# Attention over recurrent segments: E left unnormalised, outputs scaled at eviction, one tile for the values, V one round later

## The chip, the cores and the metric

The kernel runs on one core of one Trainium2 chip. The metric is the device time of one execution of the whole program in microseconds (us). Engines are named as in the profile: PE (TensorE matmuls), PEld (its weight loads), DVE (VectorE), ACT (ScalarE), POOL (GpSimd) and SP (SyncE, here only issuing DMAs). PSUM is the memory that PE writes to and that DVE and ACT read from; everything else lies in SBUF or, between stages, in DRAM.

## The reference, cut

Four layers, A, B, A, B, each added to its input after a layer norm. Layer A is attention inside segments of 32 tokens, each with 8 memory rows in front; the memory rows of a segment are the first 8 output rows of the segment before. Layer B is a linear attention over the whole sequence, which the change touches only in one copy.

```python
# layer A: x [1, 2048, 640], 32 heads of 192, 8 memory rows, segments of 32
mem = mem0
for s in range(64):
    h = concat([mem, xs[s]], axis=1)                     # 40 rows
    q, k, v = h @ Wq, h @ Wk, h @ Wv                     # per head, 192 each
    scores = q @ k.T * Dh ** -0.5
    scores = where((i < 8) | (i >= j), scores, -1e9)
    p = softmax(scores)
    o = (p @ v) @ Wo                                     # 40 rows of 640
    mem = o[:, :8]
    outs.append(o[:, 8:])
```

## The kernel before

**Layer A in two stages.** The chain carries 32 rows a segment: 8 memory rows and the first 24 tokens. Q, K and V of the last 8 tokens ("tails") depend on the layer's input alone and are projected beforehand (`A_pre`) into the DRAM arrays `kqb_d` and `vb_d`; the chain adds them as extra columns and rows, since memory rows read every key. The outputs of the tails are stored to the DRAM array `otb_d` and multiplied with Wo later, within the B layer (`post_steps`).

**The chain (`A_chain`)** goes over 64 segments one after the other, since each needs the memory rows of the one before. A segment has four rounds of 8 heads, numbered 0 to 3, in falling order in every other segment, so that weights can stay; the rest of the weights streams in from DRAM over SP's queue (`load_slot`, `load_wo`, into `arena`). The block is under `tc.manual_schedule()`: each engine runs its instructions in the order in which the code issues them, and semaphores are derived from the tiles that instructions read and write.

**One round.** `project` computes Q, K and V, 20 matmuls of 128x384 each, in four column groups of the array with 32 rows each, so a bank of PSUM holds four groups of two heads. ACT copies Q and K to `raw` (L936), DVE transposes them in blocks of 32 into `QT` and `KT` (L941, L944 to L946). `scores` adds the mask by a matmul with the identity (L963) and then six products (L968). Two heads share a block of 80x80, 32 rows of each and 16 of their tails; the mask excludes what belongs to different heads, and four blocks make 80x320. `weigh` takes the exponential (ACT, L1020), `sums` multiplies with ones (L1034), so that every row holds the column sums; `normalise` takes Ln and Exp(-x) of them on ACT (L1039, L1040) and multiplies E by the result on DVE (L1041). `attend` (L976) multiplies 80 rows of the value tile `Vs[n % 2]` with E: rows 0 to 63 are the round's values, copied from PSUM by `v_rows` (L955 on ACT, L957 on DVE), rows 64 to 79 the tails' values, which `extra_v` (L909) loads by a DMA that POOL issues. The outputs fill two PSUM banks; ACT and DVE copy the round's 64 columns to `OT` (L981, L982) and the 16 tail columns to `otb` (L988 to L991), which `store_tail` (L995, POOL) writes to DRAM. `wo_round` multiplies `OT` with the round's part of Wo into the bank `W` (48 matmuls of 128x160, L1002), summed over the four rounds.

**Two value tiles.** Round n uses `Vs[n % 2]`. Behind `attend` of round n, `tails_after(n)` calls `extra_v` for round n + 2 (or the next segment's rounds 0 and 1), into the tile that this `attend` has just read. The rows 96 to 127 of the two tiles serve as buffers for the segment's input and output rows: `load_rows` (L878) brings the next 24 rows, `hx_transpose` (L882, four instructions) puts them into `hT`, `keep_rows` (L890, four) takes the outputs from `W`, `store_rows` (L893) stores them.

**Between segments** the first 8 rows of `W` go through DVE (L1145 transposes, L1146 casts) into `hT` of the next segment. `keep_busy` (L1009) issues 14 matmuls on the identity a segment, in three groups around the last two `wo_round`s; `fill` (L1015) issues weight loads without a matmul.

**Order on PE.** Q 0, K 0, V 0; then for n = 0 to 2: Q n+1, `attend` n-1, scores n, K n+1, `sums` n, `wo_round` n-1, V n+1. At the end: scores 3, half of V 3, `attend` 2, `sums` 3, the other half, `wo_round` 2, `keep_busy`, `attend` 3, `keep_busy`, `wo_round` 3, `keep_busy`. POOL's queue holds, in this order a round: `extra_v`, the four copies of `extra_kq` (L902 to L905, tails' columns into `QT` and `KT`), `load_kqb` (L897), `store_tail`.

Of the kernel before, what the change touches and what calls it, by code (L numbers as in the profile page):

```python
# [8 lines left out]
P = 128  # L9
# [12 lines left out]
SEG_FILL = 1  # L22
# [93 lines left out]
class Kernel:  # L116
# [52 lines left out]
    def run(self, layers):  # L169
# [14 lines left out]
        self.eps = const.tile([P, 1], F32, name="eps")  # L184
# [5 lines left out]
        for li, Lt in enumerate(layers):  # L190
            last = li == len(layers) - 1
            if Lt == "A":
# [3 lines left out]
                attn = dram.tile([S, Dm], BF16, name=f"attn{li}")[:]  # L196
# [355 lines left out]
    def build_A_consts(self):  # L552
        nc, const = self.nc, self.const

        mk = const.tile([P, 80], BF16, name="mask_st")
        nc.gpsimd.memset(mk[:], MASK_NEG)

        def keep(m, base, pattern, mult):  # L560
            nc.gpsimd.affine_select(out=m, in_=m, compare_op=ALU.is_ge, fill=MASK_NEG, base=base, pattern=pattern,
                                    channel_multiplier=mult)

        for G in range(2):
            for c0, c1 in ((32 * G, 32 * G + 32), (64 + 8 * G, 72 + 8 * G)):
                nc.gpsimd.memset(mk[32 * G:32 * G + 32, c0:c1], 0.0)
            keep(mk[32 * G:32 * G + 32, 32 * G + 8:32 * G + 32], 8, [[1, 24]], -1)
            for c0 in (32 * G, 64 + 8 * G):
                m = mk[64:80, c0:c0 + 8]
                nc.gpsimd.memset(m, 0.0)  # L570
                if G == 0:
                    keep(m, 7, [[0, 8]], -1)
                else:
                    keep(m, -8, [[0, 8]], 1)
                if c0 >= 64:
                    keep(m, 8 * G, [[1, 8]], -1)
        self.mk = mk
        ones = const.tile([P, 1], BF16, name="ones_blk")
        nc.vector.memset(ones[:], 1.0)
        self.ones_blk = ones  # L580

    def layer_A(self, xn_dram, at_dram, li, x_raw=None):
# [49 lines left out]
        def load_wo(r, into=None, part=range(6)):  # L632
            t = into if into is not None else wo_end[:, :] if r in (0, 3) else wo_mid[:, 7680 * (r - 1):7680 * r]
            for k in part:
                tk = t[:, 1280 * k:1280 * k + 1280]
                if r in (0, 3):
                    self.last_load = nc.sync.dma_start(out=tk, in_=self.wo_rows[r // 3, :, 1280 * k:1280 * k + 1280])
                else:
                    nc.sync.dma_start(out=tk.rearrange("p (c m) -> p c m", m=640),
                                      in_=wov[:, 12 * r + 2 * k:12 * r + 2 * k + 2, :])  # L640
# [8 lines left out]
        def lay_out_wo(i):  # L649
            nc.sync.dma_start(out=self.wo_rows[i].rearrange("p (c m) -> p c m", m=640), in_=wov[:, 36 * i:36 * i + 12, :])  # L650
# [204 lines left out]
    def A_chain(self, xn_dram, at_dram, li, load_slot, piece, load_wo, late_wo, wo_mid, wo_end, low):  # L855
# [3 lines left out]
        with tc.tile_pool(name=f"A{li}_ch", reuse_waits="tile", bufs=1) as sp, \  # L859
# [3 lines left out]
            KT = sp.tile([P, 6, 80], BF16, name="KT")  # L863
            QT = sp.tile([P, 2, 4, 80], BF16, name="QT")
            Vs = [sp.tile([P, 896], BF16, name=f"Vp{i}") for i in range(2)]
            xr, orow = [t[96:P, 0:640] for t in Vs]
            for i, t in enumerate((KT, QT, *Vs)):
                (nc.vector if i % 2 else nc.gpsimd).memset(t[:], 0.0)
            xv = xn_dram.rearrange("(s t) d -> t s d", t=32)

# [4 lines left out]
            def load_rows(s):  # L877
                nc.gpsimd.dma_start(out=xr[8:32, :], in_=xn_dram[32 * s:32 * s + 24, :])  # L878

            def hx_transpose(hT, gs):  # L880
                for g in gs:
                    nc.vector.transpose(out=hT[32 * g:32 * g + 32, :, :],  # L882
                                        in_=xr[:, 160 * g:160 * g + 160].rearrange("p (j b) -> p b j", b=KC))
# [4 lines left out]
            def keep_rows(W):  # L888
                for g in range(4):
                    nc.scalar.activation(out=orow[:, 160 * g:160 * g + 160], in_=W[32 * g:32 * g + 32, 0:160], func=ACT.Copy)  # L890

            def store_rows(s):
                nc.gpsimd.dma_start(out=at_dram[32 * s:32 * s + 24, :], in_=orow[8:32, :])  # L893
# [6 lines left out]
            def extra_kq(kqb):  # L900
                qb = kqb[:, 96:192].rearrange("p (x i q) -> p x i q", i=3, q=16)
                nc.gpsimd.tensor_copy(out=QT[:, :, 0:4:3, 64:80], in_=qb[:, :, 0:3:2, :])  # L902
                nc.gpsimd.tensor_copy(out=QT[0:64, :, 1, 64:80], in_=qb[0:64, :, 1, :])
                nc.gpsimd.tensor_copy(out=QT[64:P, :, 2, 64:80], in_=qb[64:P, :, 1, :])
                nc.gpsimd.tensor_copy(out=KT[:, :, 64:80], in_=kqb[:, 0:96].rearrange("p (c q) -> p c q", q=16))  # L905

            def extra_v(s, n):
                r = rounds(s)[n]
                nc.gpsimd.dma_start(out=Vs[n % 2][64:80, :], in_=self.vb_d[s, r].rearrange("g t f -> (g t) f"))  # L909

            def project(hT, ps, m, n, s, steps):
# [3 lines left out]
                for i in steps:  # L915
                    b = (i + KC - ns) % KC if n == 0 else i
                    w = piece(m, r, b)
                    for g in range(4):
# [6 lines left out]
                        o = ps  # L925
                        nc.tensor.matmul(o[32 * g:32 * g + 32, 0:384], lhsT=hT[:, b, :], rhs=rhs, start=(i == 0),  # L926
# [4 lines left out]
            def values(hT, n, s, pv, steps):  # L931
                project(hT, pv, "V", n, s, steps)

            def to_raw(ps, tag):
                raw = sp.tile([P, 384], BF16, name="raw", tag=tag)
                nc.scalar.activation(out=raw[:], in_=ps[:, 0:384], func=ACT.Copy)  # L936
                return raw

            def to_rows(raw, m):
                if m == "K":  # L940
                    nc.vector.transpose(out=KT[:, :, 0:64], in_=raw[:, :].rearrange("p (c j) -> p c j", j=64))  # L941
                else:
                    rv = raw[:, :].rearrange("p (x i j) -> p x i j", i=3, j=64)
                    nc.vector.transpose(out=QT[:, :, 0:4:3, 0:64], in_=rv[:, :, 0:3:2, :])  # L944
                    nc.vector.transpose(out=QT[0:64, :, 1, 0:64], in_=rv[0:64, :, 1, :])
                    nc.vector.transpose(out=QT[64:P, :, 2, 0:64], in_=rv[64:P, :, 1, :])  # L946

            def v_rows(pv, n, which="ax"):
                for x in range(2):
                    if "ax"[x] not in which:  # L950
                        continue
                    o = self.two_heads(Vs[n % 2][0:64, 448 * x:448 * x + 448])
                    i = pv[64 * x:64 * x + 64, 0:384].rearrange("p (e f) -> p e f", e=2)
                    if x == 0:
                        nc.scalar.activation(out=o, in_=i, func=ACT.Copy)  # L955
                    else:
                        nc.vector.tensor_copy(out=o, in_=i)  # L957

            def scores():

                S = pop.tile([P, 512], F32, name="ps_s", tag="s", bufs=2)
                m = self.mk[0:80, :]
                nc.tensor.matmul(S[0:80, 0:320], lhsT=self.ident[0:80, 0:80], rhs=ap3(m, [list(m.ap[0]), [0, 4], [1, 80]]),  # L963
                                 start=True, stop=False, skip_group_check=True)
                for x in range(2):
                    for i, q0, q1 in ((0, 0, 1), (1, 1, 3), (2, 3, 4)):
                        c0 = 160 * x + (80 if i == 2 else 0)
                        nc.tensor.matmul(S[0:80, c0:c0 + 80 * (q1 - q0)], lhsT=KT[:, 3 * x + i, :], rhs=QT[:, x, q0:q1, :],  # L968
                                         start=False, stop=(x == 1 and i == 2), skip_group_check=True)
                return S  # L970

            def attend(E, n):
                O = [pop.tile([P, 512], F32, name=f"ps_o{x}", tag=f"o{x}") for x in range(2)]
                for x in range(2):
                    for k, e, i in ((0, 0, 0), (320, 1, 2), (128, 0, 1), (192, 1, 1)):
                        nc.tensor.matmul(O[x][:, 80 * i:80 * i + 80], lhsT=Vs[n % 2][0:80, 448 * x + k:448 * x + k + 128],  # L976
                                         rhs=E[0:80, 160 * x + 80 * e:160 * x + 80 * e + 80], start=(k == 0),
                                         stop=(k == 192), skip_group_check=True)
                OT = sp.tile([P, 6, 64], BF16, name="OT", tag="OT")
                o = [x[:, 0:240].rearrange("p (i q) -> p i q", q=80) for x in O]  # L980
                nc.scalar.activation(out=OT[:, 0:3, :], in_=o[0][:, :, 0:64], func=ACT.Copy)  # L981
                nc.vector.tensor_copy(out=OT[:, 3:6, :], in_=o[1][:, :, 0:64])  # L982
                return OT, o

            def keep_tail(o, late=False):
                otb = sp.tile([P, 6, 16], BF16, name="otb", tag="otb", bufs=2)
                if late:
                    nc.vector.tensor_copy(out=otb[:, 0:3, :], in_=o[0][:, :, 64:80])  # L988
                else:
                    nc.scalar.activation(out=otb[:, 0:3, :], in_=o[0][:, :, 64:80], func=ACT.Copy)  # L990
                nc.vector.tensor_copy(out=otb[:, 3:6, :], in_=o[1][:, :, 64:80])  # L991
                return otb

            def store_tail(otb, s, r):
                nc.gpsimd.dma_start(out=self.otb_d[s, :, 96 * r:96 * r + 96], in_=otb[:, :, :].rearrange("p c t -> p (c t)"))  # L995

            def wo_round(W, r, OT, first, last):
                w = wo_end[:, :] if r in (0, 3) else wo_mid[:, 7680 * (r - 1):7680 * r]
                for i in range(12):
                    c, q = i % 6, 32 * (i // 6)  # L1000
                    for g in range(4):
                        nc.tensor.matmul(W[32 * g:32 * g + 32, 0:160], lhsT=OT[:, c, q:q + 32],  # L1002
                                         rhs=w[:, 640 * i + 160 * g:640 * i + 160 * g + 160], start=(first and i == 0),
                                         stop=(last and i == 11), tile_position=(0, 32 * g), skip_group_check=True)

            def keep_busy(ps, n, w=384):

                for _ in range(n):
                    nc.tensor.matmul(ps[:, 0:w], lhsT=self.ident[:, :], rhs=wo_mid[:, 0:w], start=True, stop=True,  # L1009
# [210 lines left out]
```

## Time and profile before

| what | us |
|---|---|
| runs shown | 3728.8, 3733.5, 3735.9; median 3733.5 |
| span of the profiled execution | 3735.3 |
| mean granted clock of TensorE in it | 0.980 |
| chain of the first layer A | about 209 to 1550 |
| chain of the second layer A | about 2077 to 3420 |
| a segment, start to start, mean of 126 | 21.33 |
| shortest segment | 20.91 |
| busy in the span: PE, DVE, ACT, POOL | 3544, 2368, 2073, 1659 |
| mean DMA rate | 249 GB/s |

How to read it: the span is cut at the first and last instruction of the profiled execution. "Start" of a segment is here the end of the first of the two casts that put memory rows into `hT` (L1146). In a group's line the busy sum comes first, then the mean of one instruction in ns, then the idle time of its engine just before these instructions with what ended it. Lines of the timeline give start and duration in us; what stands in square brackets is idle time before and its releaser. A matmul's duration runs over its neighbours', since they are pipelined, so prices on PE are best taken from start to start. The landing time of a DMA counts from its issue on the engine.

### The profile page before, as it was taken

The numbers are of one execution on the slowest core, as the hardware profiler recorded it, in microseconds if no ns is written. First come the engines' busy times: TensorE is split into PE (matmuls) and PEld (weight loads), VectorE is DVE, ScalarE is ACT, GpSimd is POOL, SyncE is SP. The second block draws the span as 40 slices with busy tenths as digits, with TensorE's granted clock in tenths as the row PEclk, the third lists the DMA queues.
The fourth block names the chain that finished last, engine by engine and source line by source line (L and its number), as shares of the span: only waits on it lengthen the run. The fifth ranks groups of instructions, "written<-read, shape, count | busy, mean of one in ns | idle before, by whom it ended". The sixth has DMA issues, their size and how long they took to land.

```text
span 3735.3 us, 169098 instructions
## 1 busy us (share of the span) xinstructions
PE 3543.7 (95%) x71082; PEld 2319.9 (62%) x71390; DVE 2368.0 (63%) x6330; ACT 2073.4 (56%) x5285; POOL 1658.5 (44%) x4323
## 2 busy tenths in 40 slices
PE   9999999999999999989899999999999999999898
PEld 7766666666666666545377666666666666665453
DVE  5556666666666666456633566666666666664564
ACT  2356566666666666545423566666666666665453
POOL 3345555555555555340423455455555555553400
PEclk9999999999999999989899999999999999999899
DMA  9988788888887888910377888887887888879100
GB/s 301 326 295 294 266 289 292 275 291 278 284 294 272 293 282 276 309 57 14 137 259 216 292 279 282 283 295 275 290 282 274 289 282 289 293 268 316 58 1 29
DMA packets 531381, 931.72 MB, mean 249 GB/s; under 512 B 141034, under 2 KB 298362, under 8 KB 530618
## 3 DMA queue, kind: packets, MB, share of 16 engines
q1 hardware_dynamic: 428794, 818.87, 62.6%
q0 software_dynamic: 68160, 88.78, 8.1%
q10 hardware_dynamic: 33664, 13.24, 1.4%
q8 instruction: 558, 9.14, 1.0%
q14 instruction: 205, 1.68, 0.1%
HBM read 852.43 MB, written 72.09 MB: 248 GB/s over the span
## 4 chain that ended last, share of the span: by engine, by line
PE 35%; DVE 5%; DMA 5%; ACT 4%; issue 4%; POOL 2%; PEld 2%; SPq 0%; POOLq 0%; DVEq 0%; ACTq 0%
PE ps_qk L926 9%; PE ps_w L1002 4%; PE ps_v L926 4%; PE ps_o L976 2%; PE ps_s L968 2%; PE ps_qk L389 2%; DMA arena<-wo_rows 2%; PE ps_pre L817 1%; PE ps_s L1034 1%; DVE hT L882 1%; PEld L817 1%; PE ps_s L963 1%; PE ps_idle L1009 1%; PE ps_v L419 1%; PE kv L429 1%
## 5 line engine op out<-in xcount | busy, mean ns | idle before, releaser
L926 PEld LDWEIGHTS <-hT 128*32 128x32 bf16 x30720 | 739.4, 96 | 433.1 <-DVE hT L1146 29.0
L926 PE MATMUL ps_qk<-arena,hT 128*32 128x384 bf16 x20480 | 996.3, 327 | 12.0 <-DMA arena<-in_A_Wk_dram 2.2
L936 ACT ACTIVATE raw<-ps_qk 128x384 bf16<-128x384 f32 x1024 | 503.1, 491 | 378.3 <-PE ps_s L1034 243.9
L1002 PE MATMUL ps_w<-arena,OT 128*32 128x160 bf16 x24576 | 542.7, 235 | 38.4 <-issue 22.1
L909 POOL DMA_DIRECT2D Vp<-vb x512 | 258.8, 506 | 661.6 <-PE ps_o L976 456.4
L926 PE MATMUL ps_v<-arena,hT 128*32 128x384 bf16 x10240 | 536.6, 329 | 6.6 <-DMA arena<-in_A_Wv_dram 6.6
L1002 PEld LDWEIGHTS <-OT 128*32 128x32 bf16 x24576 | 436.2, 97 | 131.1 <-issue 53.7
L941 DVE STREAM_TRANSPOSE KT<-raw 128x384 bf16<-128x384 bf16 x512 | 296.1, 578 | 195.9 <-ACT raw L936 191.9
L944 DVE STREAM_TRANSPOSE QT<-raw 128x256 bf16<-128x256 bf16 x512 | 227.9, 445 | 239.1 <-ACT raw L936 195.9
L897 POOL DMA_DIRECT2D kqb<-kqb x512 | 291.1, 569 | 173.3 <-POOL KT L905 148.2
L957 DVE CAST Vp<-ps_v 64x384 bf16<-64x384 f32 x512 | 286.2, 559 | 98.2 <-ACT Vp L955 82.7
L995 POOL DMA_DIRECT2D otb<-otb x512 | 283.0, 553 | 116.5 <-DVE otb L991 99.0
L955 ACT ACTIVATE Vp<-ps_v 64x384 bf16<-64x384 f32 x512 | 246.3, 481 | 154.2 <-PE ps_v L926 115.4
L982 DVE CAST OT<-ps_o 128x192 bf16<-128x192 f32 x512 | 183.2, 358 | 221.2 <-PE ps_o L976 203.1
L1041 DVE TENSOR_TENSOR E<-E,ps_s 80x320 bf16<-80x320 bf16 x512 | 247.5, 483 | 73.6 <-ACT ps_s L1040 69.5
L1020 ACT ACTIVATE E<-ps_s 80x320 bf16<-80x320 f32 x512 | 221.9, 433 | 126.1 <-PE ps_s L968 97.2
L976 PEld LDWEIGHTS <-Vp 80*128 80x128 bf16 x4096 | 184.3, 99 | 154.7 <-issue 120.6
L968 PE MATMUL ps_s<-QT,KT 128*80 128x80 bf16 (+1 forms) x3072 | 233.2, 213 | 24.3 <-DVE KT L941 13.4
L976 PE MATMUL ps_o<-E,Vp 80*128 80x80 bf16 x4096 | 234.5, 202 | 22.6 <-ACT Vp L955 4.2
L981 ACT ACTIVATE OT<-ps_o 128x192 bf16<-128x192 f32 x512 | 167.8, 328 | 152.6 <-PE ps_o L976 152.3
L890 ACT ACTIVATE Vp<-ps_w 32x160 bf16<-32x160 f32 x512 | 150.7, 294 | 175.0 <-DVE wt L1145 157.9
L968 PEld LDWEIGHTS <-KT 128*80 128x80 bf16 x3072 | 194.6, 119 | 73.5 <-issue 61.4
(152 smaller groups left out, 5462.5 us busy)
## 6 DMA issues: line engine op xcount, KB each, us to landing
arena<-wo_rows SPq DMA_DIRECT2D x792, 320.0 KB, 6.8
arena<-in_A_Wq_dram SPq DMA_DIRECT2D x427, 384.0 KB, 4.6
arena<-in_A_Wv_dram SPq DMA_DIRECT2D x427, 384.0 KB, 6.4
arena<-in_A_Wk_dram SPq DMA_DIRECT2D x768, 192.0 KB, 4.8
kqb<-kqb POOLq DMA_DIRECT2D x512, 48.0 KB, 5.1
arena<-in_A_Wk_dram SPq DMA_DIRECT2D x43, 384.0 KB, 7.1
vb<-arena POOLq DMA_DIRECT2D x128, 112.0 KB, 5.9
Vp<-vb POOLq DMA_DIRECT2D x512, 28.0 KB, 4.7
```

What stands on the lines that cost most here:

```text
L897: nc.gpsimd.dma_start(out=kqb[:], in_=self.kqb_d[s, :, r, :])
L909: nc.gpsimd.dma_start(out=Vs[n % 2][64:80, :], in_=self.vb_d[s, r].rearrange("g t f -> (g t) f"))
L926: nc.tensor.matmul(o[32 * g:32 * g + 32, 0:384], lhsT=hT[:, b, :], rhs=rhs, start=(i == 0), stop=(i == KC - 1), tile_position=(0, 32 * g), ...
L936: nc.scalar.activation(out=raw[:], in_=ps[:, 0:384], func=ACT.Copy)
L941: nc.vector.transpose(out=KT[:, :, 0:64], in_=raw[:, :].rearrange("p (c j) -> p c j", j=64))
L955: nc.scalar.activation(out=o, in_=i, func=ACT.Copy)
L957: nc.vector.tensor_copy(out=o, in_=i)
L968: nc.tensor.matmul(S[0:80, c0:c0 + 80 * (q1 - q0)], lhsT=KT[:, 3 * x + i, :], rhs=QT[:, x, q0:q1, :], start=False, stop=(x == 1 and i == 2 ...
L976: nc.tensor.matmul(O[x][:, 80 * i:80 * i + 80], lhsT=Vs[n % 2][0:80, 448 * x + k:448 * x + k + 128], rhs=E[0:80, 160 * x + 80 * e:160 * x ...
L995: nc.gpsimd.dma_start(out=self.otb_d[s, :, 96 * r:96 * r + 96], in_=otb[:, :, :].rearrange("p c t -> p (c t)"))
L1002: nc.tensor.matmul(W[32 * g:32 * g + 32, 0:160], lhsT=OT[:, c, q:q + 32], rhs=w[:, 640 * i + 160 * g:640 * i + 160 * g + 160], start=(firs ...
L1041: nc.vector.tensor_tensor(out=E[0:80, 0:320], in0=E[0:80, 0:320], in1=rc, op=ALU.mult)
```

## The change

It touches `A_chain`, the masks, the layout of Wo's rows in DRAM and the copies of `post_steps`.

- E is no longer multiplied by the reciprocals of the sums. `sums` now gives them on all 128 partitions, `reciprocals` puts them into the tile `rc`, and `scale_out` multiplies the outputs by `rc` as it takes them from PSUM into `OT`: one DVE product of 128x320 for columns of whole heads, two of 64x160 for the columns that two heads share. Tail columns go to `OT` with the others and `store_tail` stores them from there; `otb` is gone.
- The outputs of `attend` lie in one PSUM bank in place of two.
- There is one value tile. It holds the tail rows of rounds of even number in rows 64 to 79, those of odd number in rows 80 to 95; `scores` and `attend` work on 96 rows, and the mask, one for each parity, excludes the other's 16.
- `OT` and the columns of `QT` hold 96 and 80 places in which round columns and tail columns change sides with the parity.
- `sums` n-1, `attend` n-1 and scores n are issued in one block; V n comes behind K n+1. `wo_round` 1, 2 and 3 come at the end of the segment. `keep_busy` is gone, `SEG_FILL` is 25 in place of 1.
- Input and output rows have tiles of their own over 128 partitions, so `hx_transpose` and `keep_rows` are one instruction each; `load_rows` and `store_rows` move 32 rows in four column groups.
- The order of rows of Wo changes with that of `OT`: `lay_out_wo` is three DMAs, `load_wo` takes rows with a step, and `post_steps` copies the tails with a step of six elements.

```diff
-            Vs = [sp.tile([P, 896], BF16, name=f"Vp{i}") for i in range(2)]
-            xr, orow = [t[96:P, 0:640] for t in Vs]
+            Vs = sp.tile([P, 896], BF16, name="Vp")
+            OT = sp.tile([P, 96, 6], BF16, name="OT")
...
             def extra_v(s, n):
                 r = rounds(s)[n]
-                nc.gpsimd.dma_start(out=Vs[n % 2][64:80, :], in_=self.vb_d[s, r].rearrange("g t f -> (g t) f"))
+                t = 64 + 16 * (n % 2)
+                nc.gpsimd.dma_start(out=Vs[t:t + 16, :], in_=self.vb_d[s, r].rearrange("g t f -> (g t) f"))
...
-            def attend(E, n):
-                O = [pop.tile([P, 512], F32, name=f"ps_o{x}", tag=f"o{x}") for x in range(2)]
+            def reciprocals(S):
+                rc = sp.tile([P, 320], F32, name="rc", tag="rc")
+                nc.scalar.activation(out=S[:, 0:320], in_=S[:, 0:320], func=ACT.Ln)
+                nc.scalar.activation(out=rc[:, :], in_=S[:, 0:320], func=ACT.Exp, scale=-1.0)
+                return rc
+
+            def attend(E):
+
+                O = pop.tile([P, 512], F32, name="ps_o", tag="o", bufs=2)
                 for x in range(2):
-                    for k, e, i in ((0, 0, 0), (320, 1, 2), (128, 0, 1), (192, 1, 1)):
-                        nc.tensor.matmul(O[x][:, 80 * i:80 * i + 80], lhsT=Vs[n % 2][0:80, 448 * x + k:448 * x + k + 128],
-                                         rhs=E[0:80, 160 * x + 80 * e:160 * x + 80 * e + 80], start=(k == 0),
+                    for k, e, c in ((0, 0, 2 * x), (320, 1, 2 * x + 1), (128, 0, 4 + x), (192, 1, 4 + x)):
+                        nc.tensor.matmul(O[:, 80 * c:80 * c + 80], lhsT=Vs[0:96, 448 * x + k:448 * x + k + 128],
+                                         rhs=E[0:96, 160 * x + 80 * e:160 * x + 80 * e + 80], start=(x == 0 and k == 0),
                                          stop=(k == 192), skip_group_check=True)
+                return O
+
+            def scale_out(O, rc, n):
+                q0 = 16 - 16 * (n % 2)
+                dst = OT[:, q0:q0 + 80, :].rearrange("p q c -> p c q")
+                rv = rc[:, :].rearrange("p (x e q) -> p x e q", e=2, q=80)
+                ov = O[:, 0:480].rearrange("p (c q) -> p c q", q=80)
+                nc.vector.tensor_tensor(out=dst[:, 0:4, :], in0=ov[:, 0:4, :],
+                                        in1=rc[:, :].rearrange("p (c q) -> p c q", q=80), op=ALU.mult)
+                for e in range(2):
+                    h = slice(64 * e, 64 * e + 64)
+                    nc.vector.tensor_tensor(out=dst[h, 4:6, :], in0=ov[h, 4:6, :], in1=rv[h, :, e, :], op=ALU.mult)
+
+            def store_tail(n, s, r):
+                q0 = 80 - 80 * (n % 2)
+                nc.gpsimd.dma_start(out=self.otb_d[s, :, 96 * r:96 * r + 96],
+                                    in_=OT[:, q0:q0 + 16, :].rearrange("p q c -> p (q c)"))
...
+                for n in range(1, L):
                     raw = q_or_k("Q", n + 1)
+                    sums(S, E)
+                    O = attend(E)
+                    tails_after(n - 1)
+                    S1 = scores(n)
+                    rc = reciprocals(S)
+                    E = weigh(S1)
+                    S = S1
+                    to_rows(raw, "Q", n + 1)
                     next_kq(s, n)
...
+                        rawk = q_or_k("K", n + 1)
+                        scale_out(O, rc, n - 1)
+                        to_rows(rawk, "K")
+                    store_tail(n - 1, s, order[n - 1])
+                    pv = values(n, pop, "v")
+                    v_rows(pv, 0, "s")
+                    v_rows(pv, 1, "s")
+                    if n < L - 1:
+                        wo_round(W, order[n - 1], n == 1, False)
...
+                pv = values(L, pqp, "qk")
+                sums(S, E)
+                O = attend(E)
                 tails_after(L - 1)
+                S1 = scores(L)
                 next_kq(s, L)
+                rc = reciprocals(S)
+                E = weigh(S1)
+                v_rows(pv, 1, "v")
+                v_rows(pv, 0, "s")
+                wo_round(W, order[L - 2], False, False)
+                sums(S1, E)
+                O1 = attend(E)
+                tails_after(L)
                 if s + 1 < NSEG:
                     hT = new_hT()
-                    hx_transpose(hT, range(1))
-                wo_round(W, order[L - 1], OT, False, False)
...
+                    hx_transpose(hT, xr)
+                scale_out(O, rc, L - 1)
+                store_tail(L - 1, s, order[L - 1])
+                wo_round(W, order[L - 1], False, False)
+                rc = reciprocals(S1)
+                scale_out(O1, rc, L)
+                wo_round(W, order[L], False, True)
+                store_tail(L, s, order[L])
                 fill(SEG_FILL)
```

## The prediction

> **What bounds the kernel now.** First the page's parts 1, 5 and 6:
>
> ```profile
> PE 3543.7 (95%) x71082; PEld 2319.9 (62%) x71390; DVE 2368.0 (63%) x6330; ACT 2073.4 (56%) x5285; POOL 1658.5 (44%) x4323
> L909 POOL DMA_DIRECT2D Vp<-vb x512 | 258.8, 506 | 661.6 <-PE ps_o L976 456.4
> L1041 DVE TENSOR_TENSOR E<-E,ps_s 80x320 bf16<-80x320 bf16 x512 | 247.5, 483 | 73.6 <-ACT ps_s L1040 69.5
> L890 ACT ACTIVATE Vp<-ps_w 32x160 bf16<-32x160 f32 x512 | 150.7, 294 | 175.0 <-DVE wt L1145 157.9
> ```
>
> PE sets the time; DVE, ACT and POOL have room. In the trace the start of a segment recurs every 21.33 us (mean of both layers; the shortest took 20.91), so 128 segments are 2,730 of the 3735.3 us. The timeline of one segment, which starts at 805.63, gives the prices on PE and the place of the value tails:
>
> ```profile
> 807.32 0.99 PE L926 MATMUL ps_v<-arena,hT 128*32 128x384 bf16 x20
> 808.13 0.99 PE L926 MATMUL ps_qk<-arena,hT 128*32 128x384 bf16 x20
> 809.05 0.33 PE L963 MATMUL ps_s<-mask_st,ident 80*80 80x320 bf16 x1
> 809.35 0.45 PE L968 MATMUL ps_s<-QT,KT 128*80 128x80 bf16 x6
> 809.73 1.00 PE L926 MATMUL ps_qk<-arena,hT 128*32 128x384 bf16 x20
> ...
> 812.82 0.45 PE L976 MATMUL ps_o<-E,Vp 80*128 80x80 bf16 x8
> 813.56 0.50 POOL L909 DMA_DIRECT2D Vp<-vb  x1 [1.85 <-PE ps_o L976]
> ...
> 817.38 0.46 PE L976 MATMUL ps_o<-E,Vp 80*128 80x80 bf16 x8
> 818.13 0.51 POOL L909 DMA_DIRECT2D Vp<-vb  x1 [1.69 <-PE ps_o L976]
> ```
>
> From start to start: a projection 0.82 us, 0.92 where a full-array product follows; mask and scores 0.30 + 0.38 (the mask 0.14 behind another full-array product); by the same view `attend` 0.28, `sums` 0.26, `wo_round` 0.84 (0.94 before a full-array product), and 1.69 from the last `wo_round` to the next segment. POOL issues the next tails (L909) 0.74 us after the start of the `attend` that frees their rows (812.82 to 813.56). The waits of PE show what these loads cost today, the view of the DMA queues, narrowed to one issue at a time, how long they are under way:
>
> ```profile
> PE ps_o L976 <- DMA Vp<-vb: 4.0, 8, 1.4
> ```
>
> ```profile
> Vp<-vb POOLq DMA_DIRECT2D x1, 28.0 KB, 5.4
> ...
> Vp<-vb POOLq DMA_DIRECT2D x1, 28.0 KB, 5.9
> ...
> Vp<-vb POOLq DMA_DIRECT2D x1, 28.0 KB, 1.9
> ```
>
> These are the issues at 813.56, 818.13 and 825.61. Sorted by place over some 122 segments, the median is 5.54 us for an issue 7.9 us into the segment (9 in 10 between 4.83 and 6.03), 5.70 at 12.5 (5.39 to 6.18), 3.54 at 16.8 and 1.95 at 19.7: the weight stream fills the DMA engines until some 17 us. PE waited for them 8 times in all, since each tile is read again only two rounds later.
>
> **The change, part by part.**
>
> **One value tile.** `attend` now reads rows 0 to 95 of it, the tail rows of both parities; the mask makes the other parity's weights zero but doesn't stop the read. `extra_v` for round n+2 is still issued behind `attend` of round n, and overwrites rows that `attend` of n+1 reads. In the built program that `attend` does wait for this load's semaphore. So two successive `attend`s stand at least 0.74 + landing + about 0.05 us apart. Call them A0 to A3, in us from the segment's start, with PE's order of the new code:
> - A0: 0.05 + three projections 2.46 + V 0.92 + scores 0.68 + K 0.82 + Q 0.92 + sums 0.26 = 6.1, taken as 6.2. Issue 6.95, landing +5.5.
> - A1 = 12.55. PE's own work from A0 (attend 0.28, scores 0.52, K and V 1.64, wo 0.84, Q 0.92, sums 0.26: 4.46) would have allowed 10.7, so PE stands 1.9. Issue 13.3, landing +5.6 (between the medians at 7.9 and 12.5).
> - A2 = 18.95. Own work 0.80 + K, V, V 2.56 + sums 0.26 = 3.62 would have allowed 16.2; PE stands 2.8. Issue 19.7, landing +1.95.
> - A3 = 21.7. Own work 0.80 + wo 0.94 + sums 0.26 = 2.0 allowed 20.95; PE stands 0.75.
> - After A3: 0.28 and `wo_round` 2, 0.84, to 22.8. `scale_out` 3 overwrites the OT that it reads, so it comes after: 0.05 + its first product on 128x320. No row shows that operation; the nearest is L1041 with 0.483, the bound above a 384-element cast, L957 with 0.559. I take 0.48, as the element count is the same; the two 64-row products lie under the first two thirds of `wo_round` 3. So 23.35, and 1.69 on: the segment takes 25.1 us at full clock, 3.75 more than before.
> What queues behind the waiting `attend` on PE: the scores of the next round, hence Exp, and the next projections; POOL's own next issue waits for `attend` too, which closes the loop.
>
> **The clock.** The profile has a stall like these:
>
> ```profile
> 1333.51 0.48 PE L968 MATMUL ps_s<-QT,KT 128*80 128x80 bf16 x6 [1.94 <-POOL KT L905]
> ```
>
> ```profile
> 1331.94:1335.35 3.41, 1.84 (x35) 1.16 (x39) 0.81 (x3) 0.91 (x3) 2.54 (x8) 1.00 0.76 278
> 1335.35:1338.77 3.42, 3.42 (x71) 3.00 (x64) 1.86 (x7) 1.54 (x5) 2.39 (x7) 0.50 0.17 41
> ```
>
> PE stood 1.57 us within one stretch of 3.41, and the granted clock (third figure from the end) was 0.50 for all of the next; gaps with 1.40 us in one stretch were followed by 1.00. The 2.8 us before A2 put over 1.6 into one stretch in most positions. A half-speed stretch loses up to 1.7 us of work; behind A1 that lies in the wait for A2, behind A2 it lies on the path for `wo_round` 1 to 3 only. Bounds 0 and 1.7; I take 0.5, a third, as the place is random: 25.6 us. The removed `keep_busy` (14 matmuls a segment, in time when PE waited) costs nothing else.
> The Trainium skill, "TensorE: Matmul & The Clock Gate", section "HAM oscillation — how this bites in real kernels", allows idle gaps up to about 3.4 us; by it no gap here would lower the clock and the segment would keep the full-clock figure. The stall above, 1.94 us long, contradicts it.
> A second page speaks against the loop: by "DMA: Bandwidth & Descriptors", section "Anatomy of one DMA — SWDGE (gpsimd) path", such a load takes 2.0 us plus bytes over 436 GB/s, here 2.07; by that the waits before A1 and A2 vanish and the weight stream would decide. The landings show it for the issue at 825.61 (1.9) and not for those under the stream (5.4, 5.9).
>
> **Unnormalised E and scaling at eviction.** L1041 (0.483), four evictions and two tail copies of DVE and ACT a round give way to three products on DVE (0.48 and, from 160 elements against 320, some 0.31 twice). A round then asks DVE for 1.59 of transposes (rows L941, L944 to L946) and 1.1 of products, ACT for 3.2 (two raw copies of 0.49, two value copies of 0.48, Exp 0.43, Ln and Exp 0.83), under at least 4.5 us of PE; on the path lies the 0.53 above. Where that cover is gone, a late product costs its 0.48, four times a segment at most: 1.9. Without E in the way, scores, sums and outputs in one block save PE some 0.1 to 0.2 us a round; it goes into the waits.
>
> **V a round later, rows, masks, DMAs.** The last V no longer splits. `hx_transpose` and `keep_rows` (four of 0.294 each, L890) become one apiece, beside PE; `keep_rows` moves ahead of Q's transposes into the time of K 0, and uncovered would cost that 0.3. POOL issues as many DMAs a segment: `load_rows` moves from behind the last `attend` to K 1 and is needed only at the next segment; `store_tail` 2 and 3 come behind the issues for A2 and A3, so they delay none of these. SP's queue issues the same `wo_rows` loads at the same places; only the layout ahead of the chain takes three DMAs for one, beside the first weights. 16 more mask instructions on POOL lie there too, beside loads; each would cost under a microsecond, once, if bare. The spread copies in the later layers read with a stride of six elements: some 1.5 us a layer, 3 in all, between 0 and 10.
>
> **Sum.** 3735.3 + 128 x (25.6 - 21.33) + 3 = 3735 + 547 + 3 = 4285 us; the median of the runs shown, 3733.5, lies 2 lower, so 4283.
>
> **Rivals.**
> - **Only the weight stream binds** (faster): if all landings were as the one at 825.61, own work would set A1 and A2 and the segment would take some 20.3 us; the stream's last packet comes at 19.43 (median) and no segment ended less than 1.35 later, so 20.8: 3735 - 68 + 3 = 3670. Decides below 2.8 us of latency at A1 and 3.7 at A0. Against it: 4.83 at the lowest twentieth.
> - **The tail store binds in place of the load**: `scale_out` 3 also overwrites rows that `store_tail` 1 reads. Issued near 15.1 and, like the store at 14.8 today, 5.09 under way, it lands at 20.2; +0.53 + 1.69 gives 22.4: 3735 + 137 + 3 = 3875. It needs the value tails not to bind, against the wait in the program.
> - **Full clock**: the same loop without the gate, 25.1: 3735 + 483 + 3 = 4221.
> - **Half clock behind every A2**: 25.1 + 1.7 = 26.8: 3735 + 700 + 3 = 4438.
>
> **Numbers.** Forecast 0.56, full clock 0.16, half clock 0.16, tail store alone 0.06, stream alone 0.05, no change 0.01. Low end: both long landings 0.5 us shorter and the full clock, 24.1, gives 4090, taken as 4085; high end 4440. The spread of the runs makes 0.2% the least that can be told from no change: faster 0.05, same 0.01, slower 0.94.
>
> **What would show it.** PE waiting at the outputs' line for Vp<-vb some 5 us a segment, 600 to 700 us in all, where it was 4.0; `attend`s 6.3, 6.4 and 2.8 us apart; landings of 5.5, 5.6 and 2.0; the granted clock at 0.50 in stretches behind A2; the wait for `otb` not the last before `scale_out` 3. Wrong: landings under 4 us while the stream runs, or `attend`s that don't wait.

## The result and the profile after

The changed kernel takes 4891 us (median of 4 runs, 4879 to 4905); the kernel before 3734 (median of 4). The ratio is 1.310 with a 95% interval of 1.307 to 1.313. The profiled execution has a span of 4892.0 us and a mean granted clock of 0.873 (before 0.980). Slower was forecast, but 4283 us and at most 4440: the loss is 1157 us where 550 were reckoned.

The page after, its busy times and the groups that answer to those shown of before (L909 is now L924, L1041 gave way to L1012 and L1016):

```profile
PE 3831.1 (78%) x69306; PEld 2480.7 (51%) x72670; DVE 2763.4 (56%) x5448; ACT 1971.6 (40%) x4405; POOL 1719.9 (35%) x4359
...
L1016 DVE TENSOR_TENSOR OT<-ps_o,rc 64x160 bf16<-64x160 f32 x1024 | 781.7, 763 | 13.8
L1012 DVE TENSOR_TENSOR OT<-ps_o,rc 128x320 bf16<-128x320 f32 x512 | 628.8, 1228 | 151.7 <-ACT rc L994 75.1
...
L924 POOL DMA_DIRECT2D Vp<-vb x512 | 258.2, 504 | 535.3 <-PE ps_o L1002 520.1
```

PE now stands, that is waits, for over a fifth of the span (5% before). The products that `scale_out` issues take 1.23 and 0.76 us. The waits of PE (in all, times, longest):

```profile
PE ps_o L1002 <- DMA Vp<-vb: 463.6, 280, 4.1
PE ps_w L1028 <- DVE OT L1012: 244.3, 265, 1.3
PE ps_w L1028 <- DVE OT L1016: 102.2, 222, 0.5
```

The first line is the forecast wait, 4.0 us in all before; the second and third were not forecast at this size. The timeline shows both, and a third thing, between A0 and A1 of one segment:

```profile
1022.47 0.45 PE L1002 MATMUL ps_o<-E,Vp 96*128 96x80 bf16 x8
...
1024.75 1.24 DVE L1012 TENSOR_TENSOR OT<-ps_o,rc 128x320 bf16<-128x320 f32 x1
1025.69 1.57 DVE L1016 TENSOR_TENSOR OT<-ps_o,rc 64x160 bf16<-64x160 f32 x2
1026.04 0.77 PE L1028 MATMUL ps_w<-arena,OT 128*32 128x160 bf16 x32 [0.69 <-DVE OT L1012]
1026.07 0.71 POOL L890 DMA_DIRECT2D xr<-xn  x1 [3.52 <-issue]
1026.78 0.50 POOL L924 DMA_DIRECT2D Vp<-vb  x1
...
1032.76 0.69 PE L1002 MATMUL ps_o<-E,Vp 96*128 96x80 bf16 x8 [3.90 <-DMA Vp<-vb]
```

A0 starts at 1022.47 and ends some 0.4 us later, but POOL issues the next tails at 1026.78, behind L890, the load of the next segment's rows, at which it had stood for 3.5 us. The landing takes until 1032.6. The trace names no releaser for this stand. In most segments it is the store of the rows before, which POOL waited for 88 times (here that store had landed at 1023.6, and what held POOL from there on stays open):

```profile
POOL xr L890 <- DMA attn<-orow: 88.9, 88, 2.2
```

The end of the segment before it:

```profile
1007.70 1.22 DVE L1012 TENSOR_TENSOR OT<-ps_o,rc 128x320 bf16<-128x320 f32 x1
...
1008.64 1.54 DVE L1016 TENSOR_TENSOR OT<-ps_o,rc 64x160 bf16<-64x160 f32 x2
...
1009.63 0.45 PE L1002 MATMUL ps_o<-E,Vp 96*128 96x80 bf16 x8 [1.68 <-DMA Vp<-vb]
...
1010.27 0.44 ACT L994 ACTIVATE rc<-ps_s 128x320 f32<-128x320 f32 x1 [1.86 <-DVE OT L1016]
...
1010.88 1.22 DVE L1012 TENSOR_TENSOR OT<-ps_o,rc 128x320 bf16<-128x320 f32 x1 [0.70 <-ACT rc L994]
...
1012.15 2.03 PE L1028 MATMUL ps_w<-arena,OT 128*32 128x160 bf16 x48 [1.10 <-DVE OT L1012]
...
1014.77 4.49 PE L940 MATMUL ps_qk<-arena,hT 128*32 128x384 bf16 x60 [0.60 <-PE L1035]
```

There is one tile `rc`, so the reciprocals of round 3 (L994) wait for the last product of round 2, and the products of round 3 for them. The three projections at 1014.77 take 4.49 us, where two took 1.81 before:

```profile
805.68 1.81 PE L926 MATMUL ps_qk<-arena,hT 128*32 128x384 bf16 x40
```

The windows of the changed kernel say why (PE busy first, the granted clock third from the end):

```profile
1007.50:1010.90 3.40, 1.73 (x71) 1.33 (x61) 2.63 (x5) 1.26 (x4) 2.46 (x9) 1.00 0.14 30
1010.90:1014.30 3.40, 2.17 (x59) 1.58 (x65) 2.52 (x4) 0.00 (x0) 1.08 (x2) 0.63 0.09 21
1014.30:1017.70 3.40, 2.93 (x40) 1.64 (x59) 1.20 (x6) 0.68 (x2) 0.11 (x1) 0.50 0.41 101
...
1017.70:1021.10 3.40, 3.40 (x71) 1.97 (x67) 1.34 (x4) 1.93 (x4) 1.00 (x3) 0.87 0.88 257
```

PE stands for 1.67 us of the first window, where `attend` of round 3 waits for its load, and for 1.23 of the second, mostly where `wo_round` 3 waits for DVE; the clock goes down behind that and stays at half over the start of the segment. Medians of the places over 124 segments, as the prediction named them, with the two decisive runs of below beside them (us from the segment's start; the last row is the mean period):

| place | predicted | changed | contiguous OT | and rows behind |
|---|---|---|---|---|
| A0 | 6.2 | 7.61 | 5.88 | 5.88 |
| A1 | 12.55 | 15.52 | 14.73 | 12.58 |
| A2 | 18.95 | 21.47 | 20.82 | 19.08 |
| A3 | 21.7 | 24.86 | 23.80 | 22.14 |
| next start | 25.1, with the clock 25.6 | 30.59 | 27.42 | 25.99 |

### The profile page after: what moved, and what is told of

The parts are those of the page before. It is cut to its first block, busy times and chain, and to the rows that moved or that the text cites. A ratio compares the mean times of both kernels' runs of the same rounds, so it can differ in the third digit from the quotient of the medians.

```text
span 4892.0 us, 167816 instructions
## 1 busy us (share of the span) xinstructions
PE 3831.1 (78%) x69306; PEld 2480.7 (51%) x72670; DVE 2763.4 (56%) x5448; ACT 1971.6 (40%) x4405; POOL 1719.9 (35%) x4359
## 4 chain that ended last, share of the span: by engine, by line
issue 29%; PE 25%; POOL 15%; DMA 13%; DVE 9%; ACT 5%; PEld 3%; POOLq 0%; DVEq 0%; SPq 0%; ACTq 0%
DMA Vp<-vb 9%; PE ps_qk L940 8%; DVE OT L1016 6%; PE ps_pre L825 3%; POOL kqb L910 3%; POOL otb L1020 2%; PE ps_o L1002 2%; POOL Vp L924 2%; PEld L1035 2%; DMA attn<-orow 2%; PE ps_w L1028 2%; PE ps_pre L849 1%; POOL KT L919 1%; POOL QT L916 1%; PE ps_qk L391 1%
## 5 line engine op out<-in xcount | busy, mean ns | idle before, releaser
L1016 DVE TENSOR_TENSOR OT<-ps_o,rc 64x160 bf16<-64x160 f32 x1024 | 781.7, 763 | 13.8
L1012 DVE TENSOR_TENSOR OT<-ps_o,rc 128x320 bf16<-128x320 f32 x512 | 628.8, 1228 | 151.7 <-ACT rc L994 75.1
L1002 PE MATMUL ps_o<-E,Vp 96*128 96x80 bf16 x4096 | 248.1, 209 | 519.9 <-DMA Vp<-vb 463.6
L1020 POOL DMA_DIRECT2D otb<-OT x512 | 281.8, 550 | 922.0 <-DVE OT L1016 898.5
L1002 PEld LDWEIGHTS <-Vp 96*128 96x128 bf16 x4096 | 201.9, 103 | 595.9 <-ACT rc L994 267.5
L924 POOL DMA_DIRECT2D Vp<-vb x512 | 258.2, 504 | 535.3 <-PE ps_o L1002 520.1
L994 ACT ACTIVATE rc<-ps_s 128x320 f32<-128x320 f32 x512 | 223.9, 437 | 358.2 <-DVE OT L1016 348.7
L983 ACT ACTIVATE E<-ps_s 96x320 bf16<-96x320 f32 x512 | 220.1, 430 | 294.7 <-PE ps_s L977 291.2
L977 PE MATMUL ps_s<-QT,KT 128*96 128x80 bf16 (+1 forms) x3072 | 259.2, 225 | 8.1 <-DVE KT L952 0.9
L993 ACT ACTIVATE ps_s<-ps_s 128x320 f32<-128x320 f32 x512 | 218.7, 427 | 110.8 <-PE ps_s L988 105.6
L977 PEld LDWEIGHTS <-KT 128*96 128x96 bf16 x3072 | 236.5, 131 | 39.2 <-issue 32.2
```

Of the source, the lines that this page charges most:

```text
L924: nc.gpsimd.dma_start(out=Vs[t:t + 16, :], in_=self.vb_d[s, r].rearrange("g t f -> (g t) f"))
L977: nc.tensor.matmul(S[0:96, c0:c0 + 80 * (q1 - q0)], lhsT=KT[:, 3 * x + i, :], rhs=QT[:, x, q0:q1, :], start=False, stop=(x == 1 and i == 2 ...
L1002: nc.tensor.matmul(O[:, 80 * c:80 * c + 80], lhsT=Vs[0:96, 448 * x + k:448 * x + k + 128], rhs=E[0:96, 160 * x + 80 * e:160 * x + 80 * e + ...
L1012: nc.vector.tensor_tensor(out=dst[:, 0:4, :], in0=ov[:, 0:4, :], in1=rc[:, :].rearrange("p (c q) -> p c q", q=80), op=ALU.mult)
L1016: nc.vector.tensor_tensor(out=dst[h, 4:6, :], in0=ov[h, 4:6, :], in1=rv[h, :, e, :], op=ALU.mult)
```

## The experiments

Twelve kernels were run, all but two in one execution each; the kernel before took 3731 to 3739 us (medians) beside them. Executions of one kernel lie up to 1% apart here (run 11: 3930 to 3967), so a difference of some 40 between two single executions says little. Times in us.

**1. No loads of tails in the chain.**

```diff
                 def tails_after(n):
-                    if n + 2 < NR:
-                        extra_v(s, n + 2)
-                    elif s + 1 < NSEG:
-                        extra_v(s + 1, n + 2 - NR)
+                    pass
```

> Leaves out the loads of the tails' values inside the chain (the tails keep the values of the first two rounds), so no attend can wait for them. If the loop of these loads is all of the loss, as the prediction had it, the time comes back to the neighbourhood of the kernel before, 3670 to 3900 us. If the three scaling products of DVE (1.23 + 0.76 + 0.76 us in the trace of the changed kernel where 0.48 + 0.31 + 0.31 were reckoned) are a second bound of their own, a segment falls only from 30.6 to about 26.0 us, and the time to about 4300: A0 near 6.2 us, 6.3 to A1 as wo_round 0 waits for DVE, 3.6 to A2, 9.9 from A2 to the end of the segment.

4482, a fall of 409. The loop is real but not all: a second bound stands. A0 to A1 is 6.22, A1 to A2 3.54 and A2 to the end 10.2 us, as reckoned from the long products (6.3, 3.6, 9.9); A0 is 7.41 and not 6.2, the low clock at the segment's start (half speed ahead of A0 in all the segments read), which was left out of that sum.

**2. Rounds 0 and 2 read 80 rows.** The weights and E of `attend` go to row 80 in even rounds, to 96 in odd ones.

```diff
-lhsT=Vs[0:96, ...], rhs=E[0:96, ...]
+kr = 80 + 16 * (n % 2)
+lhsT=Vs[0:kr, ...], rhs=E[0:kr, ...]
```

> attend of rounds 0 and 2 reads rows 0 to 79 only, so A2 and A0 no longer wait for the load behind the attend before them; A1 and A3 still do. If each wait of attend is worth what it shows (A1 to A2 5.95 us against 3.6 of PE's own work), A1 to A2 falls by 2 us or more; the load behind A2 then starts earlier, still under the weight stream, and A2 to A3 grows from 3.4 to 4.3 to 5.8: a net of 0.5 to 1.5 us a segment, 4700 to 4830 us. If the landings don't decide, 4890.

4766, as expected: A1 to A2 falls from 5.95 to 3.64, A2 to A3 grows from 3.4 to 5.1. The wait follows the rows that are read, not the tile.

**3. `load_rows` behind the load for round 2.**

```diff
-                if s + 1 < NSEG:
-                    xr = load_rows(s + 1)
                 for n in range(1, L):
...
                     tails_after(n - 1)
+                    if n == 1 and s + 1 < NSEG:
+                        xr = load_rows(s + 1)
```

> load_rows is issued behind the load of the tails' values of round 2 instead of ahead of it. In the changed kernel that load is issued 1.66 us (mean) behind A0 where 0.74 was reckoned, as POOL stands at load_rows, which waits for the store of the rows before. If that lies in the loop, A0 to A1 falls by 0.9 us and the time by 115, to about 4775; if A1 is set by something else, 4890.

4902: no gain. The tails are issued 0.74 us behind A0 as expected and A0 to A1 falls from 7.9 to 6.9, but A1 to A2 grows from 5.95 to 6.6 (the landing from 5.13 to 5.66) and A2 to the end from 9.1 to 9.5. Why all is given back isn't settled by this run; with the products short (run 6) the gain stays.

**4. Contiguous OT.** Columns of one head stand next to each other; `store_tail` and the copies of `post_steps` follow.

```diff
-            OT = sp.tile([P, 96, 6], BF16, name="OT")
+            OT = sp.tile([P, 6, 96], BF16, name="OT")
...
-                dst = OT[:, q0:q0 + 80, :].rearrange("p q c -> p c q")
+                dst = OT[:, :, q0:q0 + 80]
```

> OT is laid out by head, so the three scaling products write 80 neighbouring elements where they wrote with a step of six (12 bytes). If the step is why they take 1.23 and 0.76 us, they fall to near 0.48 and 0.31 as reckoned, A3 to the end of the segment falls from 5.7 to 3.5 to 4 us, and the time to 4480 to 4650. If it is the operands (PSUM and 32-bit in SBUF), they stay at 1.2 and 0.76 and the time at 4890.

4480, a fall of 411. The groups of this run:

```profile
L1016 DVE TENSOR_TENSOR OT<-ps_o,rc 64x160 bf16<-64x160 f32 x1024 | 324.5, 317 | 13.8
L1012 DVE TENSOR_TENSOR OT<-ps_o,rc 128x320 bf16<-128x320 f32 x512 | 251.8, 492 | 232.6 <-ACT rc L994 104.9
```

Same operands, same counts: 0.49 and 0.32 us. The step of the write was the whole of the surplus of these products. The layout changes the weight loads of `wo_round` too, but a `wo_round` at full clock takes only 0.03 us less without the step (0.81 and 0.78, from runs 9 and before), 0.1 us a segment; and it lengthens POOL's issue of the store (0.55 to 0.86 us). A3 to the end falls from 5.7 to 3.6, and A0 to 5.88: without the stands for DVE at the end, the next segment starts at full clock in 112 of 124 cases (13 in the changed kernel).

**5. Contiguous OT and no loads of tails.**

> Contiguous OT, and the loads of the tails' values left out of the chain. With each alone the time was 4480, a fall of 410. If these two are the whole loss, the rest is the prediction's second or first rival: 22.4 us a segment and 3875 us with scale_out 3 waiting for the store of tail 1, 20.8 us and 3670 with nothing but the weight stream. If something else lies in the new order, above 4000.

4000, above both figures. Neither the loop nor the long products are left, and DVE now waits for the store of the tails:

```profile
DVE OT L1012 <- DMA otb<-OT: 269.3, 155, 3.8
```

This is the prediction's second rival, at 23.5 us a segment and not 22.4: the store of tail 1 is issued at 16.5 us and not near 15.1, and lands at 20.8 and not 20.2 (medians); from there to the next start it takes 2.5 us and not 2.2.

**6. Contiguous OT and `load_rows` behind.**

> Contiguous OT, and load_rows behind the load for round 2. In the run with contiguous OT alone that load was issued 2.1 us behind A0 and A0 to A1 took 8.9 us. Theory: with the products short, the loop alone sets A1, so A0 to A1 falls to 6.5 to 7.5 us and the time by 150 to 270, to 4210 to 4330, near the predicted 4283. Rival: as in the run with this edit alone, what A1 gains is lost at A2 and A3, 4480.

4308. A1, A2 and A3 stand at 12.58, 19.08 and 22.14, 0.03, 0.13 and 0.44 us from the prediction's places. That the first two agree so closely is in part luck: A0 comes 0.3 us earlier than the 6.2 reckoned, and A0 to A1 takes 6.7 us where 6.35 was reckoned. PE waits for the tails, though less than the 600 to 700 us that the prediction asked for:

```profile
PE ps_o L1002 <- DMA Vp<-vb: 525.6, 290, 4.4
```

**7 and 10. Idle matmuls ahead of `attend`,** 20, 10 and 3 on the kernel of run 4, 10, 10 and 3 on that of run 6.

```diff
                 O = pop.tile([P, 512], F32, name="ps_o", tag="o", bufs=2)
+                for _ in range(m):
+                    nc.tensor.matmul(O[:, 0:384], lhsT=self.ident[:, :], rhs=wo_mid[:, 0:384], start=True, stop=True,
+                                     skip_group_check=True)
```

> Contiguous OT, with 20, 10 and 3 matmuls of 128x384 on the identity ahead of attend 1, 2 and 3, into the bank that attend then overwrites, to keep PE busy for some 3.2, 1.6 and 0.5 us of the 4.4, 2.5 and 1 us in which it waits. If the low clock costs time on the path, the mean clock rises from 0.91 to above 0.97 and the time falls by 0.5 to 1.0 us a segment, to 4350 to 4420. If the slow stretches lie in waits anyway, 4480 with the clock up; if the idle matmuls are in the way, above 4500.

> Contiguous OT and load_rows behind the load for round 2 (4308 us), with 10, 10 and 3 idle matmuls ahead of attend 1, 2 and 3. If the low clock (580 us of the span there) costs time on the path, as the half microsecond of the prediction had it, the time falls by some 64, to 4220 to 4270. If the slow stretches lie in the waits, it stays within 30 of 4308 though the low clock falls below 250 us.

4546 (66 more) and 4340 (32 more). The mean clock rises from 0.913 to 0.975 and from 0.933 to 0.981, the time at half clock falls from 784 to 227 us and from 580 to 167, and nothing is gained (the 32 lie within the spread): with short products the slow stretches lie in the waits for the tails, or their cost there is no larger than that of the idle matmuls (A2 to A3 grows from 3.0 to 3.5 and from 3.1 to 3.6).

**8. Staged tails, contiguous OT, a tile for the last tails.** A POOL copy of 32 rows takes the place of the wait for a landing.

```diff
+            def stage_v(s, n):
+                for k in (n, n + 1):
+                    t = 96 + 16 * (k % 2)
+                    nc.gpsimd.dma_start(out=Vs[t:t + 16, :], in_=self.vb_d[s, rounds(s)[k]].rearrange("g t f -> (g t) f"))
+
+            def place_v():
+                nc.gpsimd.tensor_copy(out=Vs[64:96, :], in_=Vs[96:P, :])
...
-                scale_out(O1, rc, L)
+                scale_to(OT[:, :, 16:80], O1, rc, 16, 80)
                 wo_round(W, order[L], False, True)
-                store_tail(L, s, order[L])
+                tail = sp.tile([P, 6, 16], BF16, name="otb", tag="E")
+                scale_to(tail, O1, rc, 0, 16)
```

> A version that keeps the changed order and the unnormalised E, with three mends: OT contiguous; the tails' values of two rounds at a time loaded into rows 96 to 127 of the value tile and put into rows 64 to 95 by one POOL copy after attend 1 and one after attend 3, so that no attend waits for a landing; the tails of round 3 scaled into a tile of their own behind wo_round 3's operands, so that scale_out 3 doesn't wait for the store of tail 1. load_rows stands behind the tail columns of round 1. If the three causes are the whole loss, the weight stream is left: 20.8 to 21.3 us a segment, 3670 to 3735. If the copy or the store still bind, 3750 to 3900.

3884, ratio 1.039 (1.037 to 1.041): the best version with the changed order, still slower than before. The copy takes 0.93 us and no `attend` waits for a landing. What PE waits for now:

```profile
PE ps_w L1033 <- issue: 91.9, 96, 3.0
PE ps_v L943 <- DMA arena<-in_A_Wv_dram: 70.7, 86, 3.5
PE ps_w L1033 <- DVE OT L1017: 68.1, 142, 1.7
```

Waits without a releaser in `wo_round`, the weights of V, and the products of `scale_out` at the end: 231 us, against an excess of 145. Segments take 22.7 us, one in ten under 21.7: the new order, mended, doesn't beat the old one. Which of these waits is worth what isn't shown.

**11. `wo_round` 1 back in the middle,** on the kernel of run 8, with `scale_out` 1 ahead of K 3's transpose.

```diff
-                    if n < L - 1:
-                        wo_round(W, order[n - 1], n == 1, False)
+                    wo_round(W, order[n - 1], n == 1, False)
...
-                wo_round(W, order[L - 2], False, False)
```

> The version with the staged tails (3884), with wo_round 1 back in the middle, behind V 2, and scale_out 1 ahead of K 3's transpose. If its loss against the kernel before lies in the three wo_rounds at the end (PE stands for issue 92 us there, 22 before), this wait falls below 40 us and the segment from 22.7 to 21.3 to 22.0: 3720 to 3810. If it lies in DVE's late scale_out or in the stream, 3850 to 3920.

3961, ratio 1.058 (1.053 to 1.064): a miss. The wait for issue stays (109.6 us), and `sums` waits 79.8 us for E. That the three `wo_round`s at the end cost this issue time isn't borne out; its cause stays open.

**12. Run 8 without the tile for the last tails.**

> The staged version without its tile for the tails of round 3, so that scale_out 3 waits for the store of tail 1 again. If this wait is worth what the prediction's rival said, about 1 us a segment, the time is 3970 to 4020, as in the run with contiguous OT and no loads (4000); if the store has landed by then, 3884.

4064, 180 above run 8 and 64 above run 5, 44 outside the expected range. The store costs 1.35 us a segment and not 1, as the stand ahead of `scale_out` 3 also brings the half clock to the next segment's start (A0 at 7.33 in place of 5.89). DVE's group says what it waits for:

```profile
L1015 DVE TENSOR_TENSOR OT<-ps_o,rc 128x320 bf16<-128x320 f32 x512 | 251.8, 492 | 365.1 <-DMA otb<-OT 275.4
```

**9. The kernel before, with its evictions writing in steps of 12 bytes.**

```diff
-                OT = sp.tile([P, 6, 64], BF16, name="OT", tag="OT")
+                OT = sp.tile([P, 64, 6], BF16, name="OT", tag="OT")
...
-                nc.vector.tensor_copy(out=OT[:, 3:6, :], in_=o[1][:, :, 0:64])
+                nc.vector.tensor_copy(out=OT[:, :, 3:6].rearrange("p q c -> p c q"), in_=o[1][:, :, 0:64])
```

> The kernel before with one edit: OT laid out by place, so that its evictions write with a step of 12 bytes, as the changed kernel's products do. If the step of the write sets the price, whatever the operation, L982 (DVE, 128x192) goes from 0.358 to some 0.7 us, and ACT's L981 from 0.328 by as much or, if this holds for DVE alone, not at all; the time rises by 0.3 to 0.7 us a segment where wo_round 3 waits for it, to 3760 to 3830. If it needs two 32-bit operands, 0.36 and 3735.

3839, and the step alone is the price, on both engines. The groups before, then in this run:

```profile
L981 ACT ACTIVATE OT<-ps_o 128x192 bf16<-128x192 f32 x512 | 167.8, 328 | 152.6 <-PE ps_o L976 152.3
L982 DVE CAST OT<-ps_o 128x192 bf16<-128x192 f32 x512 | 183.2, 358 | 221.2 <-PE ps_o L976 203.1
...
L981 ACT ACTIVATE OT<-ps_o 128x192 bf16<-128x192 f32 x512 | 418.9, 818 | 134.7 <-PE ps_o L976 134.4
L982 DVE CAST OT<-ps_o 128x192 bf16<-128x192 f32 x512 | 414.9, 810 | 205.1 <-PE ps_o L976 187.0
```

## Why the prediction was wrong

**Right: the loop.** The value tile is reused one round too early and `attend` waits for the landing. Landings at the three places are 6.25, 5.13 and 1.94 us in the changed kernel (medians) where 5.5, 5.6 and 1.95 were reckoned. Runs 1 and 5 take the loop out and gain 409 on the changed kernel and 480 us on run 4; run 12, with the tails staged, gains 244 on run 6, and run 8, with the tile for the last tails too, 424.

**Wrong, first step: the price of `scale_out`.** The prediction took 0.48 us for the product on 128x320 "as the element count is the same" and some 0.31 for those on 64x160. They took 1.228 and 0.763, because OT's layout made them write in steps of six elements; the diff showed the step, and the prediction priced by count and operands alone. Run 4 takes the step away and the prices are 0.492 and 0.317, and the time falls by 411. On the path it counts more than once: the products of rounds 2 and 3 follow each other with the reciprocals of round 3 between them, since `rc` is one tile, and the 0.53 us of the sum was only the last of this chain.

**Wrong, second step: the queue of POOL.** The prediction said that `load_rows` "moves from behind the last `attend` to K 1 and is needed only at the next segment", and asked who needs it, not what it waits for. Input and output rows now share a tile, so it waits for the store of the rows before: its issue comes 0.29 us (median) behind that store's landing. The load for round 2 is queued behind it and comes 1.66 us (mean) behind A0 instead of 0.74. With the products short, the run with `load_rows` behind gains 172 us on the run without (4480 to 4308): A0 to A1 falls by 2.0 us, 1.3 of it in the issue and 0.7 in the landing, and A1 to A2 gives 0.4 back.

So the path and the loop were right, and two terms of the sum were wrong: 0.53 us for `scale_out` on the path and 0.74 us from A0 to the issue of the next tails. These two account for 583 of the 608 us between 4283 and 4891: mended, the changed kernel takes 4308, 0.6% above the forecast, which is within the spread. They aren't independent, as run 3 shows: `load_rows` alone moved brings nothing as long as the products are long.

**The clock** was in the sum with 0.5 us behind A2, and this size holds once the two steps are mended. In run 6, 69 of 124 segments have over 0.2 us at half clock between A2 and their end, and take 7.17 us (mean) from A2 to the next start; the other 55 take 6.28, where 6.15 was reckoned at full clock. Over all segments that is 0.5 us, or some 0.4 if the later landings of those 69 (by 0.2 us) are taken off. Runs 7 and 10 gain nothing from a higher clock, but their idle matmuls lengthen A2 to A3 by 0.5 us, about as much as there is to gain. In the changed kernel the clock costs more and elsewhere, which the sum didn't have: A0 comes at 7.66 us (median) in the 111 segments with half clock ahead of it and at 5.88 in the other 13. Runs 1 and 4 tell what brings it: without the loads, and so without the stands for them, A0 stays at 7.41; without the stands for DVE at the end of the segment before, it comes at 5.88. Whether `keep_busy`, whose removal the prediction priced at nothing but the 0.5, would have kept the clock up there isn't shown: no run puts it back. The page that the prediction weighed (the Trainium skill, "TensorE: Matmul & The Clock Gate", section "HAM oscillation — how this bites in real kernels", which allows idle gaps up to some 3.4 us) was rightly set aside: stretches at 0.50 (1240 us in the changed kernel, 150 before) follow much shorter stands, 1.68 and 1.10 us in the lines above.

**The rivals.** The store of tail 1 does bind once the loop is gone (269 us of waiting in run 5; 180 us between runs 12 and 8), as the second rival said, at 4000 to 4064 rather than 3875. The weight stream alone, 3670, was not reached by any run. The 2.07 us estimated from the page on DMA (the Trainium skill, "DMA: Bandwidth & Descriptors", section "Anatomy of one DMA — SWDGE (gpsimd) path") is near what the third load took (1.94), and a third to two fifths of what the loads under the weight stream took (6.25, 5.13).

**The small terms.** No row of before prices the 3 us for the spread copies in the later layers. In the changed kernel these copies keep ACT and DVE busy for 60.0 us in place of 32.2, but the stretch behind the second chain's last start isn't longer (334.2 us, 335.3 before), nor is that between the two chains (545.6, 545.7). The 1157 us lie in the chain: 124 measured periods are 9.26 us longer, 1148 in all, and the first start comes 10 us later. In the prediction's sum some steps are rounded up: carried on from its A0 of 6.2, its own terms give 24.96 us a segment at full clock and not 25.1, which is 18 us of the 4283.

## What to carry to other kernels

An operation is priced by its access pattern as well as by its count: a bf16 write in steps of 12 bytes costs 2.3 to 2.5 times the contiguous one here, and it is visible in the diff. When an instruction moves in a queue, ask what it waits for, and who is queued behind it, before asking who needs it. A buffer that a DMA refills between two uses is in a loop with the landing time under load, so one buffer fewer may cost more than any work that it saves.

## What the runs showed of the hardware

- The extra of a write in steps of 12 bytes is 2.3 ns an element for the product on 128x320 ((1228 - 492) / 320), 2.8 for that on 64x160, 2.4 for a DVE cast and 2.6 for an ACT copy of 128x192 (run 9 and before). PE's weight loads from `OT` pay too, 124 ns at full clock with the step (run 9) and 96 without (before), but there most of it is hidden. The Trainium skill, "SBUF — State Buffer", section "Door 1: The DMA port swizzle (why `[64,N]` ≈ `[32,N]`)", tells of 16-byte lines of which at least two hits each are needed; a step of 12 bytes gives 1.33 and agrees with a penalty. Its reading that bf16 may step by 8 for free doesn't agree: a write with a step of 6 was not free.
- A higher granted clock can go with a longer time: run 7 has 0.975 and 4546 us, run 4 0.913 and 4480. The clock says little where the waits are for something else.
- A load of 28 KB landed in 1.9 to 2.7 us behind A2 and A3, when the weight stream's queue took at most 0.01 of the DMA engines' time, and in 4.7 to 6.4 behind A0 and A1, when it took 0.53 to 0.95 of it (medians by place in the changed kernel and runs 3, 4 and 6).
